# Feed-forward of an attention, mixture-of-experts and feed-forward kernel: VectorE and ScalarE take GpSimd's elementwise work, and the decoding is spread over more steps

## The chip, the cores and the metric

One core of a Trainium2 chip. The core has TensorE (matmuls), VectorE (DVE), ScalarE (ACT), GpSimd (POOL) and SyncE (SP, which only starts transfers here); each runs its own queue of instructions in order, and they wait for each other by semaphores. The metric is the device time of one execution in microseconds (us), as the median of the runs.

## The reference

Everything is float32. An attention (2 batches, 8 heads, 1152 keys, 576 pooled queries, width 64) gives 1152 tokens of 512. A routed layer sends each token to one of 8 experts. Its output goes through a feed-forward layer, the only stage that the change touches:

```python
def _moe2_ref(x, w_in, w_out):        # x 1152x512, w_in 512x2048, w_out 2048x512
    h = x @ w_in
    g = np.maximum(h, 0.0) + np.log1p(np.exp(-np.abs(h)))
    return (g @ w_out).astype(np.float32)
```

`w_in` and `w_out` reach the kernel as float64 words, which it decodes to float32 by integer operations.

## The kernel before

**Precision.** Each float32 operand is kept as two parts, `hi` (rounded for the matmul) and `lo` (the rest). `mm3` (L1450) makes one product with three matmuls: hi by hi, hi by lo, lo by hi. To split a weight tile of 128 x 1024, `split_unit` (L1363) lets ScalarE copy it to `hi` (L1370) and another engine subtract that from the tile to get `lo` (L1371); which engine, the caller says.

**Steps.** The feed-forward is a loop over 48 steps (L1831): two halves `hf` of the hidden width, three groups `g` of 384 tokens, eight columns `f` of 128 hidden units. In step n TensorE runs `h_unit` of step n (twelve matmuls of 384 columns into `fh`, three buffers) and `out_unit` of step n - 3 (nine matmuls of 512 columns into `fo`; LAG is 3). In steps 0 to 2 there is only `fh`. The softplus of a step needs, in the order of the queues:
- `softplus` (L1723): ScalarE `Abs` of `fh` into `ex` (L1726, one buffer), `Exp` (L1727), then u1 = 1 + ex on VectorE (L1729, `u` in the profile, one buffer);
- `g_split` (L1742) of the step before: ScalarE copies `ln` to `gH` (L1746), VectorE subtracts to get `gL` (L1747); TensorE's `out_unit` reads both;
- `softplus2` (L1732): ScalarE `Ln` of u1 (L1735), VectorE L1737 to L1739 (the error of u1, its subtraction, and the maximum with `fh`, which frees the buffer of `fh`).

After every eighth column `evac` copies `fo` to the five `part` tiles (first half) or adds it to them and scatters the rows to the output (second half, GpSimd, L700).

**Side work.** The rest is a list `side` of pairs of a due time (in steps) and a piece of work; after each step the loop issues all pieces that are due (L1843). So a piece's due time sets its place in every engine's queue:
- `split` of the last three early units (L1818), due at `WO_AT`, `lo` on GpSimd;
- 16 pieces of `w_in` and `w_out` of 128 x 512 words, at t = LATE0 + m x LATED: `late_load` at t - 3 (SyncE; it takes a buffer of a pool of eight, which words, `late` units and `part` tiles share), `late0` at t (ScalarE `Abs`, L1789, and a maximum on GpSimd, L1790), `late1` at t + 1 (three integer operations on VectorE, L1799 to L1801);
- `late_split` of the eight units so made (two pieces each), LATE2 steps after a unit's second piece, and for units 5 to 7 not before LATE3, LATE3 + 1.5, LATE3 + 3; `lo` on GpSimd;
- `place` (nine scatters of token places by GpSimd, due from step 18) and `tok_load` (step 27).

The earlier decoding of other weights, during the attention, has the same maximum on VectorE (L171).

Of the kernel before, what the change touches and what calls it, by code (L numbers as in the profile page):

```python
# [9 lines left out]
F32 = mybir.dt.float32  # L10
# [3 lines left out]
AF = mybir.ActivationFunctionType  # L14
# [7 lines left out]
def tile_attn_moe_ffn(  # L22
# [13 lines left out]
    nc = tc.nc  # L36
# [26 lines left out]
    NHIP = 4  # L63
    NHIP2 = 5
    LATE0 = 2.0
    LATED = 1.347
    LATE2 = 2.527
    LATE3 = 25.778
    LATES = 1.5
    WO_AT = (0.0, 1.0, 3.0)  # L70
    X0B = 3
# [126 lines left out]
    ff_units = []  # L198
# [4 lines left out]
    late_units = ff_units[N_EARLY:]  # L203
# [7 lines left out]
    right = {}  # L211
# [62 lines left out]
    lt = ap1.tile([P, NCH, H, E], F32, name="lt")  # L274
# [1088 lines left out]
    def split_unit(u, r, eng, pool=None, keep=None):  # L1363
        pool = pool or (hipA if u[0] in ("w2", "wo") or keep is not None else right["hip"])
        if keep is None or ("hi", keep) not in fixed:
            a = pool.tile([P, 1024], F32R, tag="hi", name="hi")
            b = pool.tile([P, 1024], F32R, tag="lo", name="lo")
        if keep is not None:
            a, b = fixed.setdefault(("hi", keep), (a, b) if ("hi", keep) not in fixed else None)
        nc.scalar.copy(a, r)  # L1370
        eng.tensor_tensor(b, r, a.bitcast(F32), op=ALU.subtract)  # L1371
        hi[u], lo[u] = a, b
# [333 lines left out]
    hip2 = ctx.enter_context(tc.tile_pool(name="hip2", bufs=NHIP2, reuse_waits="tile"))  # L1706
# [16 lines left out]
    def softplus(g, f):  # L1723
        t = fh.pop((g, f))
        ex = fp.tile([P, GT], F32, tag="ex", name="ex", bufs=1)
        nc.scalar.activation(ex, t, AF.Abs)  # L1726
        nc.scalar.activation(ex, ex, AF.Exp, scale=-1.0)  # L1727
        u1 = fp.tile([P, GT], F32, tag="u1", name="u1", bufs=1)
        nc.vector.tensor_scalar_add(u1, ex, 1.0)  # L1729
        sp[g, f] = t, ex, u1  # L1730

    def softplus2(g, f):  # L1732
# [17 lines left out]
    fo, part, lt = {}, {}, {}  # L1750
# [33 lines left out]
    def late0(m):  # L1784
        t = words[m]
        a = fp.tile([P, 512], I32, tag="dec_a", name="dec_a", bufs=2)
        w = t.rearrange("p (n w) -> p n w", w=2)
        dec[m] = a, w[:, :, 1], w[:, :, 0]
        nc.scalar.activation(a.bitcast(F32), w[:, :, 1].bitcast(F32), AF.Abs)  # L1789
        nc.gpsimd.tensor_scalar_max(a.bitcast(F32), a.bitcast(F32), 2.0 ** -15)  # L1790

    def late1(m):
        a, top, low = dec.pop(m)
# [8 lines left out]
                                       op1=ALU.bitwise_or)  # L1802

    def late_split(m):
        split_unit(late_units[m], lt.pop(m), nc.gpsimd, hip2 if m < NHIP2 else right["hip"])

    split(ff_units[4], nc.vector)
    seq = [(hf, g, hf * 8 + f) for hf in range(2) for g in range(NG) for f in range(8)]
# [5 lines left out]
    def fat(t, f, *a):  # L1814
        side.append((t, len(side), f, a))

    for m in range(5, N_EARLY):
        fat(WO_AT[m - 5], split, ff_units[m], nc.gpsimd)  # L1818
    for m in range(2 * len(late_units)):
        t = LATE0 + m * LATED  # L1820
        fat(max(t - 3, 0), late_load, m)
        fat(t, late0, m)
        fat(t + 1, late1, m)
    for m in range(len(late_units)):
        t = LATE0 + (2 * m + 1) * LATED + LATE2
        fat(t if m < NHIP2 else max(t, LATE3 + LATES * (m - NHIP2)), late_split, m)
    for c in range(NCH):
# [3 lines left out]
    for n in range(len(seq)):  # L1831
        h_unit(*seq[n][1:])
        if n >= LAG:
            out_unit(*seq[n - LAG], (2, 0, 1) if seq[n - LAG][2] % 8 == 7 else range(CPG))
        if n >= LAG:
            evac((2,), *seq[n - LAG])
        softplus(*seq[n][1:])
        if n:
            g_split(*seq[n - 1][1:])
        softplus2(*seq[n][1:])  # L1840
        if n >= LAG:
            evac((0, 1), *seq[n - LAG])
        while side and side[0][0] < n + 1:  # L1843
            _, _, f, a = side.pop(0)
            f(*a)
# [38 lines left out]
```

## Time and profile before

| | |
|---|---|
| median of 3 runs | 684.07 us (682.27 to 684.11) |
| profiled execution | 681.26 us |
| span of it, first to last instruction | 679.4 us |
| mean granted TensorE clock | 0.988 |
| busy in the span: PE, DVE, ACT, POOL | 627.0, 527.4, 383.8, 323.1 us |

PE is TensorE's matmuls, PEld its weight loads (one for each matmul, and they overlap). A group of instructions shows count, busy time and mean duration; "idle before, releaser" is the time that the engine stood before them and what ended it. `x <- y` means that x is computed from y.

### The profile page before, as it was taken

The page shows a single profiled execution, that of the slowest core. Times are in us where ns is not written, and L with a number is a line of the kernel's source. Part 1 is how long each engine was busy: PE and PEld are TensorE (multiplying, and loading weights), DVE is VectorE, ACT ScalarE, POOL GpSimd, SP SyncE. Part 2 cuts the span into 40 slices and gives each one's busy share as a digit, 9 for nine tenths or more (in the row PEclk, how much of TensorE's full clock was granted, in tenths as well). Part 3 has the DMA queues.
Part 4 walks back from the last instruction along what each step waited for, and adds up shares of the span by engine and source line. Part 5 has one row for each costly group of instructions (what it writes and reads, how often), then busy time and mean ns, then how long its engine had stood idle before and what let it go on. Part 6 is the DMA issues. An engine that isn't in the chain of part 4 may idle for free. (4 is left out here: it accounts for less than half of the span.)

```text
span 679.4 us, 11733 instructions
## 1 busy us (share of the span) xinstructions
PE 627.0 (92%) x3995; PEld 505.6 (74%) x3995; DVE 527.4 (78%) x1000; ACT 383.8 (56%) x865; POOL 323.1 (48%) x255
## 2 busy tenths in 40 slices
PE   6997999999998999988899999999989999999996
PEld 4664666666665766667888889998778778999995
DVE  6899878887988897788937544656999999877664
ACT  4656376667665676663535443555566655754441
POOL 3666676877676876458352100023544564402021
PEclk9999899999998999998999999999999999999999
DMA  5884557585846452049778979974212212001011
GB/s 156 200 211 125 181 143 238 168 245 163 234 116 184 117 150 78 20 152 308 229 262 293 368 256 319 324 257 157 66 59 64 92 34 29 2 1 46 1 47 46
DMA packets 65665, 104.34 MB, mean 154 GB/s; under 512 B 21720, under 2 KB 35928, under 8 KB 65600
## 3 DMA queue, kind: packets, MB, share of 16 engines
q1 hardware_dynamic: 63248, 96.72, 46.6%
q0 software_dynamic: 2352, 6.82, 2.8%
q8 instruction: 33, 0.54, 0.4%
q14 instruction: 32, 0.26, 0.1%
HBM read 75.26 MB, written 16.02 MB: 134 GB/s over the span
## 5 line engine op out<-in xcount | busy, mean ns | idle before, releaser
L513 POOL TENSOR_TENSOR acc<-acc,pt 128x512 f32<-128x512 f32 (+1 forms) x100 | 149.2, 1492 | 40.5 <-ACT pt L476 36.4
L476 ACT ACTIVATE pt<-st 128x256 f32<-128x256 f32 (+1 forms) x288 | 110.1, 412 | 60.4 <-PE st L474 50.7
L421 DVE TENSOR_REDUCE mxt<-mx 128x1 f32<-128x384 f32 (+1 forms) x213 | 107.2, 549 | 23.6 <-PE mx L420 22.2
L472 PE MATMUL st<-QA,KA 128*128 128x256 f32 (+1 forms) x288 | 93.1, 330 | 7.6 <-ACT pt L476 7.5
L474 PE MATMUL st<-QB,KB 128*128 128x256 f32 (+1 forms) x288 | 84.0, 297 | 1.2 <-ACT QB L452 0.9
L490 PE MATMUL pv<-pt,vn 128*64 128x256 f32 (+1 forms) x576 | 83.4, 424 | 1.3 <-ACT pt L476 1.3
L420 PE MATMUL mx<-KA,QA 128*128 128x384 f32 (+1 forms) x192 | 70.2, 385 | 8.2 <-DVE mxt L421 5.0
L472 PEld LDWEIGHTS st<-QA,KA 128*128 128x128 f32 x288 | 54.6, 190 | 20.2 <-ACT pt L476 17.5
L1451 PE MATMUL fh<-x2H,hi 128*128 128x384 f32 x192 | 66.3, 345 | 1.3 <-DVEq L1676 1.3
L1453 PE MATMUL fh<-x2H,lo 128*128 128x384 f32 x192 | 64.8, 337 | 0.0
L1452 PE MATMUL fh<-x2L,hi 128*128 128x384 f32 x192 | 64.7, 337 | 0.0
L1453 PE MATMUL fo<-hi,gL 128*128 128x512 f32 x144 | 57.2, 397 | 6.2 <-DVE gL L1747 6.2
L490 PEld LDWEIGHTS pv<-pt,vn 128*64 128x64 f32 x576 | 38.2, 140 | 29.8 <-issue 6.1
L1371 POOL TENSOR_TENSOR lo<-raw,hi 128x1024 fp32r<-128x1024 f32 x7 | 16.9, 2422 | 87.9 <-ACT hi L1370 87.9
L420 PEld LDWEIGHTS mx<-KA,QA 128*128 128x128 f32 (+1 forms) x192 | 35.4, 190 | 30.6 <-DVE mxt L421 13.7
L1452 PE MATMUL fo<-lo,gH 128*128 128x512 f32 x144 | 56.4, 392 | 0.0
L1451 PE MATMUL fo<-hi,gH 128*128 128x512 f32 x144 | 56.4, 392 | 0.0
L474 PEld LDWEIGHTS st<-QB,KB 128*128 128x128 f32 x288 | 54.7, 190 | 2.0 <-ACT QB L452 1.2
L1735 ACT ACTIVATE ln<-u 128x384 f32<-128x384 f32 x48 | 25.2, 525 | 44.1 <-DVE u L1729 43.8
L1371 DVE TENSOR_TENSOR lo<-raw,hi 128x1024 fp32r<-128x1024 f32 x37 | 44.2, 1221 | 7.6 <-ACT hi L1370 6.9
L1452 PE MATMUL y<-hL,hi 128*128 128x256 f32 x160 | 44.9, 280 | 2.4 <-DVE hL L1475 2.4
L1726 ACT ACTIVATE ex<-fh 128x384 f32<-128x384 f32 x48 | 23.5, 489 | 41.4 <-PE fh L1453 36.0
(332 smaller groups left out, 1572.2 us busy)
## 6 DMA issues: line engine op xcount, KB each, us to landing
raw<-in_moe_w_dram SPq DMA_DIRECT2D x72, 512.0 KB, 5.3
words<-in_moe_w_in_dram SPq DMA_DIRECT2D x16, 512.0 KB, 5.2
words<-in_moe_w_out_dram SPq DMA_DIRECT2D x16, 512.0 KB, 3.6
xs<-zt SPq DMA_DIRECT2D x13, 528.0 KB, 4.2
vn<-in_v_dram SPq DMA_DIRECT2D x8, 576.0 KB, 6.1
qn<-in_q_dram SPq DMA_DIRECT2D x16, 256.0 KB, 5.3
wf<-dec_o SPq DMA_DIRECT2D x16, 256.0 KB, 2.1
raw<-wf SPq DMA_DIRECT2D x8, 512.0 KB, 4.5
```

The source lines that it names most:

```text
L420: nc.tensor.matmul(m[0:n, 0:GT], QA[i][:, h, j * P:j * P + n], KA[i][:, h, x], start=True, stop=True)
L421: nc.vector.tensor_reduce(out=mxt[i][0:n, j, h, g:g + 1], in_=m[0:n, 0:GT], axis=AX.X, op=ALU.max)
L472: nc.tensor.matmul(st[:, 0:n], ka[:, h, c * P:(c + 1) * P], qa[:, h, q0:q1], start=True, stop=False)
L474: nc.tensor.matmul(st[:, 0:n], kb[:, h, c * P:(c + 1) * P], qb[:, h, q0:q1], start=False, stop=True)
L476: nc.scalar.activation(pt_t[s][:, h, 0:n], st[:, 0:n], AF.Exp)
L490: nc.tensor.matmul(o[h * 64:(h + 1) * 64, 0:n], vn[i][:, h, c - k, :], pt_t[s - k][:, h, 0:n], start=(c == k), stop=(c - k == NKC - 1))
L513: eng.tensor_tensor(a, a, pt_t[s][:, :, 0:n], op=ALU.add)
L1371: eng.tensor_tensor(b, r, a.bitcast(F32), op=ALU.subtract)
L1451: nc.tensor.matmul(o, a, b, start=first, stop=False)
L1452: nc.tensor.matmul(o, a, bl, start=False, stop=False)
L1453: nc.tensor.matmul(o, al, b, start=False, stop=last)
L1735: nc.scalar.activation(ln, u1, AF.Ln)
```

## The change

Four edits, all in the feed-forward stage. The `lo` subtraction of the three early units and of the eight late ones moves from GpSimd to VectorE, and so does the maximum of `late0`. The "plus one" of the softplus moves from VectorE to ScalarE. The decoding's pace LATED goes from 1.347 to 1.8 steps a piece, so that the last piece is due at step 29, not 22.2, and LATE3 goes from 25.778 to 24.2. The late units 5, 6 and 7 are then split at 24.3, 27.9 and 31.5 (before: 25.8, 27.3, 28.8).

```diff
-    LATED = 1.347
+    LATED = 1.8
-    LATE3 = 25.778
+    LATE3 = 24.2
...
-        nc.vector.tensor_scalar_add(u1, ex, 1.0)
+        nc.scalar.activation(u1, ex, AF.Copy, bias=1.0)
...
-        nc.gpsimd.tensor_scalar_max(a.bitcast(F32), a.bitcast(F32), 2.0 ** -15)
+        nc.vector.tensor_scalar_max(a.bitcast(F32), a.bitcast(F32), 2.0 ** -15)
...
-        split_unit(late_units[m], lt.pop(m), nc.gpsimd, hip2 if m < NHIP2 else right["hip"])
+        split_unit(late_units[m], lt.pop(m), nc.vector, hip2 if m < NHIP2 else right["hip"])
...
-        fat(WO_AT[m - 5], split, ff_units[m], nc.gpsimd)
+        fat(WO_AT[m - 5], split, ff_units[m], nc.vector)
```

## Rows read from the trace of the kernel before

**Rows 1.** Stretches of 20 steps each: length, then busy time by engine, clock, DMA.
```profile
480.05:574.48 94.43, 88.22 (x421) 74.06 (x420) 89.12 (x150) 53.92 (x103) 48.88 (x39) 1.00 0.23 62
578.64:662.68 84.04, 84.04 (x422) 76.12 (x420) 61.13 (x112) 44.09 (x89) 15.50 (x16) 1.00 0.06 20
```

**Rows 2.** Waits from 480.05 to 574.48: total us, times, longest us.
```profile
PEld fo L1453 <- DVE gL L1747: 9.4, 8, 1.8
PE fo L1453 <- DVE gL L1747: 6.2, 7, 1.3
PEld fh L1451 <- DVE ln L1739: 5.1, 13, 0.4
```

**Rows 3.** Groups of VectorE by line from 461.14 on.
```profile
L1738 DVE TENSOR_TENSOR ln<-ln,u 128x384 f32<-128x384 f32 x48 | 27.7, 576 | 1.7
L1739 DVE SCALAR_TENSOR_TENSOR ln<-fh,ln 128x384 f32<-128x384 f32 x48 | 26.8, 558 | 1.7
L1737 DVE SCALAR_TENSOR_TENSOR u<-u,ex 128x384 f32<-128x384 f32 x48 | 26.8, 557 | 3.8 <-ACT ln L1735 0.6
L1747 DVE TENSOR_TENSOR gL<-ln,gH 128x384 fp32r<-128x384 f32 x48 | 26.6, 554 | 2.8 <-ACT gH L1746 2.2
L1729 DVE TENSOR_SCALAR u<-ex 128x384 f32<-128x384 f32 x48 | 24.2, 504 | 20.4 <-ACT ex L1727 19.6
L1799 DVE TENSOR_SCALAR dec_a<-dec_a 128x512 int32<-128x512 int32 x16 | 17.6, 1097 | 0.0
L1800 DVE SCALAR_TENSOR_TENSOR dec_b<-words,dec_a 128x512 int32<-128x512 int32 x16 | 12.5, 783 | 0.5
L1801 DVE SCALAR_TENSOR_TENSOR late<-words,dec_b 128x512 int32<-128x512 int32 x16 | 11.1, 692 | 0.6
L1772 DVE COPY part<-fo 128x512 f32<-128x512 f32 x3 | 2.0, 681 | 0.0
```

**Rows 4.** Durations of two lines, least, median and most, in ns.
```profile
L1729 DVE TENSOR_SCALAR u<-ex x48: 350/360/1775, 464.6 to 666.1; 128x384 f32<-128x384 f32 x48
L171 DVE TENSOR_SCALAR dec_a<-dec_a x16: 408/934/1726, 33.7 to 275.8; 128x512 f32<-128x512 f32 x16
```

**Rows 5.** The order of time, GpSimd and VectorE: start us, duration us.
```profile
477.76 2.47 POOL L1371 TENSOR_TENSOR lo<-raw,hi 128x1024 fp32r<-128x1024 f32 x1 [1.19 <-ACT hi L1370]
...
478.48 2.04 DVE L1799 TENSOR_SCALAR dec_a<-dec_a 128x512 int32<-128x512 int32 x1
...
484.78 0.42 DVE L1799 TENSOR_SCALAR dec_a<-dec_a 128x512 int32<-128x512 int32 x1
```

**Rows 6.** Groups of VectorE and ScalarE from 461.14 on.
```profile
L1371 DVE TENSOR_TENSOR lo<-raw,hi 128x1024 fp32r<-128x1024 f32 x1 | 1.2, 1226 | 1.5 <-ACT hi L1370 1.5
...
L1727 ACT ACTIVATE ex<-ex 128x384 f32<-128x384 f32 x48 | 25.2, 525 | 1.6
L1746 ACT CAST gH<-ln 128x384 fp32r<-128x384 f32 x48 | 24.3, 506 | 4.2 <-DVE ln L1739 2.9
L1726 ACT ACTIVATE ex<-fh 128x384 f32<-128x384 f32 x48 | 23.5, 489 | 41.4 <-PE fh L1453 36.0 <-DVE u L1737 4.2
```

**Rows 7.** The order of time at the first step, TensorE and VectorE.
```profile
461.14 0.41 PE L1451 MATMUL fh<-x2H,hi 128*128 128x384 f32 x1 [1.26 <-DVEq L1676]
...
465.56 0.56 DVE L1737 SCALAR_TENSOR_TENSOR u<-u,ex 128x384 f32<-128x384 f32 x1 [0.59 <-ACT ln L1735]
```

**Rows 8.** The order of time in the tail, ScalarE, VectorE and TensorE.
```profile
666.47 0.53 ACT L1735 ACTIVATE ln<-u 128x384 f32<-128x384 f32 x1
...
669.42 0.56 DVE L1747 TENSOR_TENSOR gL<-ln,gH 128x384 fp32r<-128x384 f32 x1 [0.64 <-ACT gH L1746]
...
670.16 0.39 PE L1453 MATMUL fo<-hi,gL 128*128 128x512 f32 x1
```

**Rows 9.** DMA issues (KB each, median us to landing), and the only table load.
```profile
words<-in_moe_w_out_dram SPq DMA_DIRECT2D x8, 512.0 KB, 3.5
...
L89 ACT ACT_TABLE_LOAD  x1: 1283/1283/1283, 0.9 to 0.9; - x1
```

## The prediction

> **What bounds the kernel now.** I read the stretches first, then the waits, then the groups by line, then single instructions.
>
> The change touches only the feed-forward stage, 48 steps from 461.14 us on [rows 7]. One step of TensorE is twelve `fh` and nine `fo` matmuls, 21 weight loads. Both stretches of [rows 1] hold 420 weight loads, so both are 20 whole steps: 6 to 25 and 27 to 46, counted from 0. The first takes 94.43 us, the second 84.04 us, with the granted clock at 1.00, its upper level (2.4 GHz), in both. So 84.04 / 20 = 4.202 us is TensorE's own step, and steps 6 to 25 carry 94.43 - 84.04 = 10.39 us above it. That is all that this stage can give back: steps 0 to 5 (18.91 us) are three of `fh` alone and three of about 4.2, and steps 26 to 47 run at TensorE's pace already.
>
> What holds TensorE in steps 6 to 25? [Rows 2] name VectorE: `fo` waits for `gL` (9.4 us by the weight loads, 6.2 by the matmuls, overlapping), `fh` for `ln` (5.1 us). And VectorE is busy 89.12 of 94.43 us there, against 61.13 of 84.04 later [rows 1]. It is full, so the question is what it spends its time on.
>
> [Rows 3] show two groups whose mean is no property of the work. The softplus' "plus one" (L1729) has a mean of 504 ns, but 360 in the median and 1775 at most [rows 4]. The decoding's mask-and-shift (L1799) has a mean of 1097 ns. [Rows 5] show why: at 478.48 it starts while GpSimd's `lo` subtraction runs (477.76 to 480.23) and lasts 2.04 us, 0.29 beyond that one's end; at 484.78, with no subtraction running, it takes 0.42. So a one-input VectorE instruction that meets a GpSimd subtraction stands until it is over. The two-input ones hardly do: `gL` 554 and L1737 557 ns in the mean of 48 [rows 3].
>
> **The change, part by part.** VectorE first, in clean durations, in the 20 steps 6 to 25.
> - Softplus without the "plus one": 0.557 + 0.558 + 0.558 (L1738, clean value taken from its neighbours) + 0.554 = 2.227 a step [rows 3], 44.5 us.
> - Decoding, a piece every 1.8 steps, not 1.347: eleven pieces fall here, before all sixteen. L1799 0.42 [rows 5], L1800 0.69 (its mean of 0.783 holds stretched ones; I take that of L1801, which is of the same shape), L1801 0.692 [rows 3], and the maximum, now on VectorE. No row shows it in this stage; L171 is the same operation and shape, 0.408 at least, 0.934 in the median, 1.726 at most [rows 4], among GpSimd's attention work. I take 0.41, since GpSimd is left with scatters here and L1799 of this shape takes 0.42 beside light GpSimd work; 0.41 and 1.73 stay as ends. Piece 2.21, eleven 24.3 us.
> - Splits: VectorE's takes 1.226 [rows 6]. Six late ones here, 7.4 us. The three of `WO_AT` come in steps 0, 1 and 3.
> - Two copies of `part`, 0.681 each [rows 3]: 1.4 us.
>
> Sum 77.6 us, below TensorE's 84.04. VectorE stops being the bound, and the 10.39 us go.
>
> ScalarE takes the "plus one": 128x384 on it lasts 0.489 (`Abs`), 0.525 (`Exp`) or 0.506 (`gH`) [rows 6]; I take 0.51, ends 0.49 and 0.53. ScalarE was busy 53.92 us [rows 1]; 20 x 0.51 makes it at most 64.1 of 84.04, fewer with the pieces that move out. The Trainium skill, "ScalarE: Activation LUTs", What ACT_TABLE_LOAD costs, prices an activation with immediate bias at 186 ns + 0.833 per element, 506 ns here, and about 93 ns more where the bias is a pointer operand; by that the instruction would take 0.60, and the tail below would lose 0.09 us more; no row here has such a bias.
>
> *The new waits.* `u1` has one buffer, so ScalarE's write waits for L1738 of the step before, and behind it stand `gH` and `Ln`. But `Abs` of the same step already waits for L1737, and `Abs` and `Exp` (1.01 us) cover the 0.56 of L1738. VectorE in turn no longer waits for itself but for `Ln`: from one L1737 to the next goes 0.557 + 0.489 + 0.525 + 0.51 + 0.506 + 0.53 = 3.12 us, under 4.20.
>
> *The first steps* are where VectorE could still be late: three steps of `fh` alone pass at half length, and three splits fall there. Up to the end of `gL` of step 6 VectorE has 7 x 2.227 + 4 splits (4.9) + 3 maxima (1.2) + 3 x 1.81 = 27.1 us, from 465.6 [rows 7]: 492.7. I allow 1.2 more for its waits on ScalarE there (an estimate, about half of the 2.55 us of ScalarE's five instructions): 493.9. TensorE asks for it in step 9, since `fo` runs three steps behind: at 461.14 + 6.3 (the three short steps: 480.05 - 461.14 - 3 x 4.202) + 6 x 4.202 + 2.6 (twelve `fh` and two `fo`, an estimate: a little over half a step) = 495.2. It holds, with 1.3 us to spare; afterwards VectorE gains 0.3 us a step.
>
> *What moves.* Late loads and decoding go later. SP carries only these loads here, and they land in 3.5 us [rows 9], three steps (12.6 us) before `Abs` needs them. At step 26 the pool of eight is full (five `part`, two word tiles, one late unit), so the last load waits for the decoding of that step; it is needed in step 29, and it costs nothing. The last split, in step 31, ends 2.1 (`fh`) + 2.56 (ScalarE) + 1.67 (L1737 to L1739) + 1.23 = 7.6 us after that step's start, and is used in step 33, 2 x 4.2 + 2.1 = 10.5 us after it. GpSimd's nine placing scatters lose the maxima between them; their result is needed only from step 35.
>
> *The tail.* After the last `fh` nothing hides ScalarE: `Ln` [rows 8] comes 0.43 to 0.53 us later, since "plus one" ran on VectorE under `gH` and now stands in ScalarE's queue. `gL` ends 669.98 and its matmul starts at 670.16, so 0.18 is slack; I count +0.3 us.
>
> Sum: -10.4 + 0.3 = -10.1 us against the profiled execution's 681.26 (span 679.4): 671.2. The median of the runs shown is 684.07, 2.8 above it; the stage that changes is the same, so I forecast 684.07 - 10.1 = **674.0 us**.
>
> **Rivals.**
> - *VectorE stays the bound for a while.* For: only 1.3 us to spare at step 9. If the maximum costs L171's median of 0.934 [rows 4], eleven add 5.7 us: 83.3 of 84.04, so no catching up, and three early ones (1.6 us) overrun the 1.3. At its 1.73 eleven add 14.5: 92.1, and 2.3 us of the gain are left. Against: GpSimd has no tensor work left here. By the two prices 675 to 682, say 678.
> - *The change doesn't do what it says*, because it is not GpSimd that stretches VectorE. Then L1799 keeps its 1.097 and the maximum takes its 0.934: 77.6 + 7.4 + 5.7 = 90.7 for steps 6 to 25, and steps 26 to 31, which now decode too, only keep pace. Gain 94.43 - 90.7 - 0.3 = 3.4: 680.7. Against: [rows 5], where the long one ends with GpSimd's subtraction.
> - *Slower: ScalarE reloads its table at each "plus one".* One load took 1.283 us [rows 9]; away and back is 2.57 a step. ScalarE's step, 64.1 / 20 = 3.2, becomes 5.8 during the decoding and at least 5.1 after it: 32 x 5.8 + 16 x 5.1 = 267 us, where 209 pass now from 461.14 to the 670.16 of [rows 8]: 742. It decides from "plus one" above 1.5 us, where ScalarE's step passes 4.2. Against: the whole trace holds one table load [rows 9], among copies, `Abs`, `Exp` and `Ln`. The Trainium skill, "ScalarE: Activation LUTs", Table sets, says that cheap functions (copy, abs) are in every set; by that it does not happen, and the one load agrees.
>
> **Chances.** Forecast 0.83, with a range of its own of 671.2 to 677; VectorE early 0.08; not GpSimd 0.05; table loads 0.03; the rest, 0.01, lies anywhere. Within 0.3% (about what runs of this kernel can tell from no change, 2 us) only a part of the third case and of the rest falls: 0.03. Slower 0.04, faster 0.93. The range goes from 671.0, where every step is as short as step 26 (578.64 - 574.48 = 4.16 us between the stretches of [rows 1]), the tail loses nothing and a run falls somewhat below the median, to 679.0, through most of the first rival.
>
> **What would show it.** Right: steps 6 to 25 take 84 to 85 us; `fo` waits on `gL` for under 1 us there; L1799 has a mean near 0.42 and the maximum near 0.41; VectorE is about 92% busy in these steps; ScalarE's "plus one" lasts 0.49 to 0.53 (0.60 would be the pointer price); one table load. Wrong: a maximum or L1799 near 1 us without GpSimd (second rival); waits on `gL` between steps 6 and 12 (first rival); more table loads; or a word load that lands after `Abs` asks for it, which would show as ScalarE idle before L1789.

## The result, and the profile after

Right after the prediction the changed kernel took 674.35 us in the median of 4 runs (672.72 to 675.87), the kernel before beside it 684.09 (4 runs, 682.27 to 685.63): a ratio of 0.9858 (95% interval, as for all ratios here, 0.9830 to 0.9885). Twice more the same code ran beside the experiments: 681.88 us (11 runs, ratio 0.9952, 0.9929 to 0.9974) and 680.29 us (9 runs, 0.9929, 0.9898 to 0.9959). So the kernel is faster in all three, but by 9.7 us once and by 2.3 and 4.9 us later. Its 24 runs fall into two groups: 6 at 672.7 to 675.9, 18 at 678.7 to 683.4. The forecast of 674.0 lies in the smaller group; 17 of the 18 others lie above the range's 679.0. The reason, as far as one profile of the smaller group and two of the larger show it, is one thing that the prediction had dismissed, GpSimd's scatters; where they hurt differs from run to run.

The profiled execution of after took 675.87 us (span 674.1, mean granted clock 0.982), 5.39 below that of before. The feed-forward, from its first `fh` matmul to the start of its last `fo` matmul, went from 211.83 us (461.14 to 672.97) to 203.52 (463.87 to 667.39), 8.31 less; it began 2.73 us later, which is no delay: in the kernels below whose code is the same up to there and which show none it begins between 458.8 and 464.3.

Steps 6 to 25 of after, and the next 20 steps but one, in the columns of [rows 1]:

```profile
482.77:568.47 85.70, 83.42 (x422) 75.76 (x421) 76.14 (x140) 65.73 (x131) 1.06 (x1) 1.00 0.26 75
572.63:656.67 84.04, 84.04 (x422) 76.13 (x421) 55.04 (x100) 52.15 (x108) 6.96 (x12) 1.00 0.07 26
```

94.43 became 85.70, VectorE 89.12 became 76.14. The second stretch is as long as before, 84.04. The waits of the first stretch, to be held against [rows 2]:

```profile
POOL tok L981 <- DMA td<-tokid,pos: 17.3, 1, 17.3
ACT ex L1726 <- DVE u L1737: 12.8, 12, 2.0
DVE gL L1747 <- ACT gH L1746: 5.4, 7, 1.5
ACT dec_a L1789 <- DMA words<-in_moe_w_in_dram: 5.1, 1, 5.1
PEld fo L1451 <- ACT gH L1746: 2.6, 1, 2.6
...
PE fo L1451 <- ACT gH L1746: 2.3, 1, 2.3
```

The 9.4 us of `fo` on `gL` are gone. What is left of TensorE's waiting is one wait of 2.3 us on ScalarE's `gH`, and ScalarE had stood 5.1 us for a load of words. Least, median and most of the lines of [rows 4, 5], and of the new ones:

```profile
L1799 DVE TENSOR_SCALAR dec_a<-dec_a x16: 416/418/421, 481.5 to 591.7; 128x512 int32<-128x512 int32 x16
L1790 DVE TENSOR_SCALAR dec_a<-dec_a x16: 416/417/427, 476.7 to 588.1; 128x512 f32<-128x512 f32 x16
L1729 ACT ACTIVATE u<-ex x48: 522/525/532, 467.3 to 660.1; 128x384 f32<-128x384 f32 x48
```

None of these lines of VectorE is stretched any more. The one long step is step 6, 6.86 us. In the order of time, ScalarE and then TensorE:

```profile
484.72 0.66 ACT L1789 ACTIVATE dec_a<-words 128x512 f32<-128x512 f32 x1 [5.11 <-DMA words<-in_moe_w_in_dram]
...
486.77 0.49 ACT L1746 CAST gH<-ln 128x384 fp32r<-128x384 f32 x1
...
487.32 0.50 PE L1451 MATMUL fo<-hi,gH 128*128 128x512 f32 x1 [2.28 <-ACT gH L1746]
```

`Abs` of the words stands ahead of the softplus in ScalarE's queue, so `gH` came late. Why were the words late? GpSimd in order of time, the first and the last of its nine `td` scatters, and the DMA from 463.8 to 486:

```profile
457.21 1.09 POOL L700 DMA_INDIRECT td<-tokid,pos  x1 [1.86 <-DMA xs<-xn,slot]
...
468.12 0.97 POOL L700 DMA_INDIRECT td<-tokid,pos  x1 [0.80 <-DMA td<-tokid,pos]
```

```profile
DMA  0909000992967224138899961055694299995992
GB/s 1 30 0 15 15 0 15 52 30 7 30 15 22 7 7 22 15 89 295 355 429 392 207 22 37 22 44 74 96 74 74 103 118 118 104 103 59 96 81 22
...
words<-in_moe_w_in_dram SPq DMA_DIRECT2D x7, 512.0 KB, 19.6
```

In the kernel before, these scatters ran from 544.8 to 572.2, because GpSimd's subtractions and maxima stood in front of them. With these gone the queue was empty and they ran at 457, beside the first seven loads of words, which landed after 19.6 us in the median (4.6 in the same stretch of before). The DMA line is busy tenths in 40 slices: many slices are nine tenths busy at 15 to 118 GB/s, where others move 392 and 429.

The other group of runs has the delay elsewhere. The order of time around the stage's start in the third measurement of the same code (label e5_after), ScalarE, GpSimd's last scatter, TensorE (its last matmul ahead of the stage and the first in it), and then two stretches, the first 2.5 us of the stage and its steps 0 and 1:

```profile
458.21 0.37 ACT L1503 CAST x2H<-y 128x256 f32 x1 [1.37 <-PE y L1453]
466.85 0.37 ACT L1503 CAST x2H<-y 128x256 f32 x1 [8.27 <-remote]
...
465.76 0.96 POOL L700 DMA_INDIRECT td<-tokid,pos  x1 [0.21 <-issue]
...
460.54 0.28 PE L1453 MATMUL y<-hH,lo 128*128 128x256 f32 x1
468.10 0.66 PE L1451 MATMUL fh<-x2H,hi 128*128 128x384 f32 x1 [7.28 <-issue]
```

```profile
468.10:470.60 2.50, 2.50 (x8) 2.50 (x9) 1.22 (x1) 1.04 (x1) 0.00 (x0) 0.50 0.97 13
...
468.10:474.90 6.80, 6.80 (x25) 6.80 (x25) 1.62 (x2) 3.53 (x6) 0.00 (x0) 0.59 0.84 20
```

ScalarE's last copy ahead of the stage normally comes 2.42 us after the end of the one before it; here 8.27, so 5.85 us late. TensorE stood for 7.28 us and then ran at a granted clock of 0.50, the lower level (1.2 GHz), and 0.59 in the mean of steps 0 and 1, which took 6.80 us instead of 4.24 (e1_hold below). Its scatters ran from 455.42 to 466.72. Here the words still landed in time, and step 6 took 4.15 us. The trace of e0_after shows the same: 9.75 us instead of 2.42.

### The profile page after: what moved, and what is told of

Same layout as the page of the kernel before. It is cut to its first block, busy times and chain, and to the rows that moved or that the text cites. A ratio compares the mean times of both kernels' runs of the same rounds, so it can differ in the third digit from the quotient of the medians.

```text
span 674.1 us, 11763 instructions
## 1 busy us (share of the span) xinstructions
PE 624.1 (93%) x3995; PEld 509.8 (76%) x3995; DVE 507.6 (75%) x979; ACT 404.2 (60%) x913; POOL 267.8 (40%) x228
## 5 line engine op out<-in xcount | busy, mean ns | idle before, releaser
L421 DVE TENSOR_REDUCE mxt<-mx 128x1 f32<-128x384 f32 (+1 forms) x213 | 107.2, 548 | 21.7 <-PE mx L420 20.3
L490 PE MATMUL pv<-pt,vn 128*64 128x256 f32 (+1 forms) x576 | 82.0, 418 | 1.3 <-ACT pt L476 1.3
L700 POOL DMA_INDIRECT out_dram<-part,tok x9 | 9.3, 1037 | 172.1 <-DVE part L1777 171.5
L1371 DVE TENSOR_TENSOR lo<-raw,hi 128x1024 fp32r<-128x1024 f32 x40 | 47.9, 1222 | 7.8 <-ACT hi L1370 7.2
L1747 DVE TENSOR_TENSOR gL<-ln,gH 128x384 fp32r<-128x384 f32 x48 | 26.7, 556 | 35.9 <-ACT gH L1746 35.9
```

The lines of the kernel that those rows point to most:

```text
L421: nc.vector.tensor_reduce(out=mxt[i][0:n, j, h, g:g + 1], in_=m[0:n, 0:GT], axis=AX.X, op=ALU.max)
L490: nc.tensor.matmul(o[h * 64:(h + 1) * 64, 0:n], vn[i][:, h, c - k, :], pt_t[s - k][:, h, 0:n], start=(c == k), stop=(c - k == NKC - 1))
L1747: nc.vector.tensor_tensor(b, ln, a.bitcast(F32), op=ALU.subtract)
```

## The experiments

The kernels ran in three groups, each with the kernel before beside it (684.19, 684.21 and 685.2 us). "Stage" is the span from the first `fh` to the last `fo` matmul's start in the profile; the loss or gain is read there first, since the time ahead of the stage varies by some us.

**e0_after, e5_after: the changed kernel itself.**

> The changed kernel once more, beside the variants below. Both theories: ratio to before about 0.986; the feed-forward stage (first fh to last fo matmul) about 203.5 us, step 6 about 6.9 us long with ScalarE waiting some 5 us for a word load, the word loads of w_in landing some 20 us after issue.

681.88 us; stage 202.48. It missed: ScalarE stood for no load of words, but 7.3 us longer than normal ahead of the stage (9.75 less 2.42), as in the trace just shown.

> The changed kernel once more, unchanged, to see which of its two delays it has here. Theory A (the scatters freed early collide with loads wherever they are then): either ScalarE waits for words in step 6 (a stage of 203 to 204 us, 673 to 676 us) or the stage begins 8 to 10 us late at the branch ahead of it (679 to 683 us); in both the scatters lie at 454 to 470 us, and the kernel with GpSimd's maxima in the same call is faster by 3 to 11 us. Rival B (the difference between the two medians so far is the chip's, not the kernel's): the kernel before moves by the same amount, and the ratio is that of the kernel with GpSimd's maxima within 0.3%.

680.29 us; stage 203.19, started 5.85 us late. The kernel before moved by 1.0 us only, and the kernel with GpSimd's maxima beside it (e4 below) took 673.49, so the second median is no drift of the chip.

**e1_hold: the scatters held back.**

```diff
+    def hold():
+        nc.gpsimd.tensor_copy(dm, held_by[0][0:1, 0:1])   # reads one number of step 18's ln
+    fat(TD0, hold)
     for c in range(NCH):
         fat(TD0 + 0.6 * c, place, c)
```

> The changed kernel, with one small GpSimd copy of a value that VectorE makes in step 18 ahead of the nine placing scatters, so that they can't run before that step. Theory A (the scatters, no longer behind GpSimd's tensor work, run at the stage's start and delay the word loads beside them): the word loads land in 4 to 6 us, ScalarE no longer waits for them, step 6 takes 4.15 us, the stage is 2.4 us shorter than in the changed kernel (about 201.1 us), ratio to before about 0.982. Theory B (the first word loads are late for another reason, such as their place in SyncE's queue): step 6 stays near 6.9 us and the stage near 203.5.

672.93 us (6 runs, 668.64 to 675.49), ratio 0.9828 (0.9795 to 0.9862); stage 200.78. GpSimd stood 85 us at this copy:

```profile
537.12 0.18 POOL L1830 COPY dm<-ln 1x1 f32<-1x1 f32 x1 [85.09 <-DVE ln L1740]
537.47 1.10 POOL L700 DMA_INDIRECT td<-tokid,pos  x1 [0.18 <-issue]
```

No step is long, no load makes ScalarE wait, and neither delay occurs. One instruction that only orders GpSimd's queue is worth 9.0 us against e0_after in the same group. None of the 30 runs of the six kernels whose scatters come late (e1, e2, e3, e4, p6, p7) takes more than 677.33 us; 18 of the 24 of after take 678.7 or more. The early scatters are the cause of both delays.

**e2_max_gp: the maxima back on GpSimd**, which then hold the scatters as before.

```diff
-        nc.vector.tensor_scalar_max(a.bitcast(F32), a.bitcast(F32), 2.0 ** -15)
+        nc.gpsimd.tensor_scalar_max(a.bitcast(F32), a.bitcast(F32), 2.0 ** -15)
```

> The changed kernel with the maxima of the decoding back on GpSimd. They stand ahead of the scatters in GpSimd's queue again. Theory A: no wait for words, step 6 near 4.2 us, the stage near 201 to 202 us. Theory B: as the changed kernel, 203.5. On the stretching of VectorE: if only GpSimd's two-input subtraction holds one-input VectorE work, L1799 has a mean of 0.42 to 0.6 us here; if any GpSimd tensor work does, it is near 1 us and VectorE becomes late (fo waits for gL by several us).

671.79 us, ratio 0.9807 (0.9782 to 0.9831), the lowest median of all, though its interval overlaps e1's; stage 200.81, scatters from 532.85. So this part of the change gains nothing, and by freeing the scatters it costs what they cost. L1799 stays at 419 ns in the median (642 at most), but that tests little, for it meets only one maximum here. Other instructions of VectorE that begin while GpSimd's maximum of 1.6 us runs are held for a part of it:

```profile
474.74 1.49 POOL L1790 TENSOR_SCALAR dec_a<-dec_a 128x512 f32<-128x512 f32 x1 [20.24 <-DVE u L1737]
474.76 1.01 DVE L1738 TENSOR_TENSOR ln<-ln,u 128x384 f32<-128x384 f32 x1
```

L1738 takes 1.01 us, not 0.56, and ends before the maximum does. VectorE has room for this here: no step gets longer.

**e3_hold_tail, e4_max_gp_tail: the last step's plus-one on VectorE**, on top of e1 and of e2.

```diff
+        if (g, f) == seq[-1][1:]:
+            nc.vector.tensor_scalar_add(u1, ex, 1.0)
+        else:
             nc.scalar.activation(u1, ex, AF.Copy, bias=1.0)
```

> As the variant that holds the scatters, and the plus one of the very last step alone is on VectorE again. Both theories of the tail: if ScalarE's extra instruction ahead of the last Ln costs the 0.3 to 0.44 us between the last h_unit and the end, these come back: from the last step's first fh to the last fo matmul 10.3 us, not 10.7; otherwise no difference to the variant that only holds the scatters. Total about 0.3 us below that variant.

> The changed kernel with the maxima back on GpSimd and the plus-one of the last step alone on VectorE. Theory A (the scatters must stay late, and the tail loses 0.4 us to ScalarE's queue): scatters from about 533 us, no wait of ScalarE for words, steps 6 to 25 in 83.0 to 83.2 us, the stage 200.3 to 200.6 us, about 671.4 us, ratio 0.979 to 0.982. Rival B (the tail's 0.4 us is no part of the time, since the last evacuations wait for something else): the stage as with the maxima alone, 200.8 us.

673.31 us (ratio 0.9833, 0.9809 to 0.9858) and 673.49 us (0.9825, 0.9797 to 0.9852). The stage fell to 200.36 and 200.38, so the 0.42 us of the tail comes back in both profiles; in the time it cannot be seen.

**p1_u1_only, p2_pace_only, p3_split_only: one part of the change alone**, in the kernel before: the plus-one on ScalarE; the two pace constants; the splits on VectorE (the diff's lines of each, and no others).

> The kernel before, with only the plus one of the softplus moved to ScalarE. GpSimd keeps its subtractions, so L1799 still meets them. Theory A (what bounds the stage is VectorE's load per step, and GpSimd's subtraction is a part of that load through the one-input instruction that meets it): VectorE's step is 2.227 + (1.10 + 0.78 + 0.69) / 1.347 = 4.14 us, just under TensorE's 4.15, so most of the gain comes from this part alone: stage 202 to 205 us (before 211.8), L1799 with a mean of 1.0 to 1.3. Theory C (the parts add up, each by the VectorE time it takes away: 20 x 0.36 to 0.50 us here): stage 204 to 205 and the other parts add the rest. If the stage stays above 208, VectorE's load is not what the sum made it.

> The kernel before, with only the decoding's pace and LATE3 changed (1.8 steps a piece). Theory A: VectorE's step is 2.227 + 0.50 + (1.10 + 0.78 + 0.69) / 1.8 = 4.16 us, about TensorE's 4.15, so this part alone gives most of the gain too: stage 202 to 206 us. Theory C: less VectorE work in steps 6 to 25 but the same work in all, spread over more steps: 5 pieces x 2.6 us less there, stage about 204 if nothing comes back in steps 26 to 31, 208 or more if it does.

> The kernel before, with only the eleven subtractions moved from GpSimd to VectorE; the maxima stay on GpSimd, pace and plus one as before. Theory A: no one-input VectorE instruction near 2.0 us any more, L1799 with a mean of 0.42 to 0.6, the plus one never above 0.6; VectorE's step is 2.227 + 0.36 + 1.80 / 1.347 + 1.226 / 2.694 = 4.38 us, still over TensorE's 4.15, so about 20 x 0.23 = 4.6 us of the loss stay: stage 204 to 207. Theory D (the long one-input instructions come from something else than GpSimd's subtraction, such as the maxima or ScalarE): L1799 keeps a mean near 1 us and the stage gets longer, 212 to 216, since VectorE has 13.5 us more to do.

| | time, us | ratio (95%) | stage | L1799 mean, ns |
|---|---|---|---|---|
| before | 684.2 | 1 | 211.83 | 1097 |
| plus-one | 682.81 | 0.9994 (0.9966 to 1.0023) | 212.58 | 1109 |
| pace | 683.85 | 1.0000 (0.9964 to 1.0036) | 213.09 | 953 |
| splits | 680.57 | 0.9959 (0.9934 to 0.9983) | 208.21 | 559 |

Theory A's 202 to 205 for the plus-one was wrong by far: alone it is worth nothing. VectorE's groups of that kernel show a part of the reason, and a line of ScalarE the larger part:

```profile
L1738 DVE TENSOR_TENSOR ln<-ln,u 128x384 f32<-128x384 f32 x48 | 33.3, 693 | 1.7
...
L1799 DVE TENSOR_SCALAR dec_a<-dec_a 128x512 int32<-128x512 int32 x16 | 17.7, 1109 | 0.0
...
569.59 0.66 ACT L1789 ACTIVATE dec_a<-words 128x512 f32<-128x512 f32 x1 [4.90 <-DMA words<-in_moe_w_out_dram]
```

GpSimd's subtractions are still there and now also hold L1738, whose two inputs both lie in SBUF (`fh` and `fo` lie in PSUM, the memory of TensorE's results; the other tiles here lie in SBUF): 693 ns in the mean instead of 576, 2.73 us at most. That makes step 3 1.76 us longer than before. The larger loss is the scatters once more: the last load of words was issued at 556.7, among them (544.2 to 573.0), and ScalarE stood for it until 569.59, so that step 25 took 8.06 us, 3.90 too many. With the tail's 0.43 these outweigh the 5.4 us that the other steps of 6 to 25 gained. With the pace alone, steps 6 to 25 fell from 94.43 to 89.59 us, but steps 27 to 46 rose from 84.04 to 90.02, the "comes back" of theory C; 3.7 us of it lie in step 33 (7.91 us), for which GpSimd's last subtraction ended too late:

```profile
PEld fo L1452 <- POOL lo L1371: 2.3, 1, 2.3
PE fo L1452 <- POOL lo L1371: 2.0, 1, 2.0
```

Only the splits alone gained, 3.6 us of stage, less than the 4.8 to 7.8 expected (204 to 207). No subtraction of GpSimd is left in that kernel, and VectorE is still busy for 85.57 of the 90.96 us of steps 6 to 25, now with its own work and the maxima's holding (L1799 meets seven of them and takes 0.42 to 1.12 us there):

```profile
488.08:579.04 90.96, 87.38 (x422) 74.18 (x421) 85.57 (x153) 55.48 (x108) 33.55 (x32) 1.00 0.24 53
```

Three gains of -0.75, -1.26 and 3.62 us add up to 1.6; with the scatters held, all parts together give 11.05. So they do not add up. (The maxima alone were not run.)

**p6_hold_split_gp, p7_hold_no_u1: one part undone**, in e1_hold: the splits back on GpSimd; the plus-one back on VectorE.

> The changed kernel with the scatters held until step 18, and the splits' subtractions back on GpSimd. Theory A (a GpSimd subtraction holds the VectorE instruction that meets it for up to 2 us): VectorE sheds 6 x 1.23 = 7.4 us in steps 6 to 25 and gains about 6 x 1.6 = 9.6 us of holding, 78.3 of 83.0, so it keeps up on the average: the stage 201 to 204 us, with single steps of 4.5 to 6 us beside the subtractions. Rival B (the edits' gains add up): the splits' part alone gave 3.6 us, so the stage is 204.4 us or more.

> The changed kernel with the scatters held until step 18, and the plus-one back on VectorE. Theory A (VectorE's clean sum decides): it is busy 76.1 + 20 x 0.36 = 83.3 us in steps 6 to 25, as much as TensorE's 83.0, and starts behind: the stage 201.5 to 204.5 us, so the plus-one is worth 1 to 4 us once the rest is done. Rival B (the plus-one is worth nothing, as when it was moved alone): the stage 200.3 to 200.9 us, the tail's 0.4 us included.

673.40 us (4 runs, ratio 0.9848, 0.9806 to 0.9890; stage 202.79) and 674.14 us (4 runs, 0.9849, 0.9818 to 0.9879; stage 202.42). Both stages are as theory A said, 2.01 and 1.64 us above e1 (2.06 for the second without the tail, which it gets back). So once the rest is done, the splits and the plus-one are worth 2 us of stage each, in one profile of each; the ratios, against e1's 0.9828, cannot tell them from nothing. Steps 6 to 25 of both, p6 and then p7:

```profile
480.60:563.56 82.96, 82.96 (x422) 75.90 (x420) 76.87 (x130) 60.22 (x121) 23.40 (x24) 1.00 0.28 64
```

```profile
479.77:563.47 83.70, 83.69 (x422) 75.68 (x421) 79.17 (x155) 52.47 (x100) 11.86 (x19) 1.00 0.29 63
```

In both VectorE is under TensorE's 83 us (p7's 79.17 is not the 83.3 of its theory A), and the steps run at TensorE's pace but for single stalls: steps 3 and 33 of p6 (5.92, 4.49 us), steps 16 and 33 of p7 (4.60, 5.65). In p7 the largest is step 33, outside the stretch that the theory named: TensorE waits 1.17 us for the last split's `lo`. Step 3 of p6 is one subtraction and one two-input instruction of VectorE, in the order of time:

```profile
468.77 2.39 POOL L1371 TENSOR_TENSOR lo<-raw,hi 128x1024 fp32r<-128x1024 f32 x1 [0.85 <-ACT hi L1370]
...
468.84 2.73 DVE L1739 TENSOR_TENSOR ln<-ln,u 128x384 f32<-128x384 f32 x1
```

(L1739 here is L1738 of before.) It ends at 471.57, 0.41 after GpSimd's end, and lasts 2.17 longer than its 0.56.

**d1_dummy: GpSimd kept busy to no purpose.** In e1_hold, two subtractions whose result nobody reads, beside each late split.

```diff
         split_unit(late_units[m], lt.pop(m), nc.vector, ...)
+        for _ in range(2):
+            nc.gpsimd.tensor_tensor(idle, right["H"][:, 0, 0:960].bitcast(F32), hi[late_units[m]][:, 0:960].bitcast(F32), op=ALU.subtract)
```

> The variant of the changed kernel that holds the scatters, with two idle subtractions (128 x 960, about 2.3 us each) on GpSimd added at each of the eight late splits; nothing uses their result. Theory A: one-input VectorE instructions (L1790's and L1799's successors in this kernel) that meet one last up to 2 us or more, in at least four of the steps with a split; all others stay at 0.42, and the two-input instructions stay within 0.1 us of 0.56 and 0.69; the stage is 0 to 2 us longer than 200.8, since VectorE has some slack. Theory D: all one-input instructions stay at 0.42 to 0.43.

694.59 us, ratio 1.0159 (1.0112 to 1.0205); stage 222.46, 21.7 us above e1. The expectation of 0 to 2 us was wrong by an order. The split on VectorE, here and (second fence) in e1:

```profile
L1371 DVE TENSOR_TENSOR lo<-late,hi 128x1024 fp32r<-128x1024 f32 x8 | 23.3, 2912 | 0.0
```

```profile
L1371 DVE TENSOR_TENSOR lo<-late,hi 128x1024 fp32r<-128x1024 f32 x8 | 9.7, 1215 | 0.0
```

16 idle subtractions of 2.54 us stretch the eight splits from 1.22 to 2.91 us each, and the mask-and-shift (L1799, here L1802) to 0.81 in the mean; `fo` waits for `gL` again, 10.1 us in all. The expectation that two-input instructions stay as they are failed too: besides the splits, one `gL` took 2.58 us. It is the plainest proof that GpSimd's subtraction itself, without any data that someone needs, holds VectorE. That this alone was what the kernel before suffered from is not shown: p3 takes the subtractions away and keeps 7.4 of the 11.05 us, and p6 keeps them and is only 2.01 above e1. By these two, what filled VectorE was the sum of its own work and the holding.

## Why the prediction was right, and where it was wrong

*What bounds the kernel, and the size of the gain.* VectorE was the bound of steps 6 to 25, and it stopped being that: right. The size was off: TensorE's step is not 4.202 us. In e1 it takes 4.15 in steps 4 to 23, 4.16 to step 28, and later 4.22, but 4.16 in steps 35, 36, 43 and 44; the undisturbed steps of the other kernels do the same, except in d1 (4.19 early, 4.14 late). So [rows 1] gave the mean of later steps, and 20 earlier ones need 82.96 us, as e1 shows: 11.47 us could go, 1.08 more than the 10.39. The prediction had step 26 with its 4.16 and used it for the end of its range alone. Why some steps take 0.07 more was not tested.

*VectorE's sum.* 77.6 us forecast, 76.14 measured (75.71 in e1). L1799 0.42 and the maximum 0.41: 0.418 and 0.417. The first steps held: in steps 6 to 25 of e1, where nothing else delays them, TensorE never waits for VectorE. The rivals "VectorE stays the bound" and "not GpSimd" fall by this, the latter also by d1.

*"The two-input ones hardly do."* Wrong as a rule. L1738 with 2.73 us beside a subtraction of 2.39 (p6), and `lo` with 2.91 instead of 1.22 (d1), show that those with both inputs in SBUF are held as long. What misled the reading: in the kernel before none of these began inside a subtraction. The lines around the subtraction of [rows 5], in the order of time:

```profile
477.41 0.56 DVE L1738 TENSOR_TENSOR ln<-ln,u 128x384 f32<-128x384 f32 x1
477.76 2.47 POOL L1371 TENSOR_TENSOR lo<-raw,hi 128x1024 fp32r<-128x1024 f32 x1 [1.19 <-ACT hi L1370]
478.00 0.56 DVE L1739 SCALAR_TENSOR_TENSOR ln<-fh,ln 128x384 f32<-128x384 f32 x1
```

Beside all eleven subtractions of that trace L1738 had begun before, and kept its 0.56. L1739, one of whose inputs (`fh`) lies in PSUM, began inside all eleven and took 0.56 too, so for that kind the prediction was right. The Trainium skill, "SBUF — State Buffer", Who interferes with whom, says that a VectorE instruction with two SBUF inputs contends with a GpSimd instruction that reads SBUF, and that the order of issue decides who waits. The rows of p6 and d1, where the subtraction came first, and the L1738 shown here, which came first itself, agree; the prediction had read averages instead. It changed no term of the sum, since the subtractions left GpSimd, but it is a part of why the plus-one alone is worth nothing: the holding passes to the next in line that can be held.

*ScalarE's plus-one.* 0.51 forecast within 0.49 and 0.53; 0.526 measured, not the 0.60 of a pointer operand. One table load, so the slower rival falls.

*"What moves."* This is the step that failed. "GpSimd's nine placing scatters lose the maxima between them; their result is needed only from step 35" asked when the scatters are needed, not when they can start. Their due time, step 18, sets their place in GpSimd's queue and nothing else; with the work in front of them gone, they began 88 us earlier (457.21, not 544.8), into the loads of words. That the loads "land in 3.5 us" was the median of eight, seven of which were issued before the first scatter: 19.6 in the first trace, for the seven beside the scatters. The sign of it, ScalarE idle before L1789, was named, but priced at nothing.

*The tail.* +0.3 forecast, +0.43 measured, and 0.42 given back in e3.

*The sum of the first trace.* In steps 6 to 25, -10.39 forecast, -8.73 measured: 1.04 more from the shorter step (20 x 4.15 against 84.04) and 2.71 lost in step 6 (6.86 - 4.15). With the tail's +0.43 that is -8.30. Two errors of opposite sign left this only 1.8 us off the forecast -10.1, and the first four runs were all of the smaller group: that their median lies at 674.35 is luck. (It lies 9.7 us below that of before; where the 1.4 us beyond the stage's 8.3 lie is not shown.) In the larger group of runs the loss is 8 to 9 us: 5.85 or 7.3 of standing, and about 2.4 or 1.7 of slower first steps (the stages of e5 and e0 against e1's 200.78), which fits the 9.0 us between the medians of e0 and e1.

*Open.* What stood ahead of the stage. The profile calls what ScalarE waited for at L1503 remote, but the copy waits for one semaphore only, which TensorE's last `y` matmul raises. By the semaphore events of the traces it rises at 466.83 in e5 and 467.77 in e0, 6.0 and 7.6 us after the recorded end of that matmul (460.82 and 460.17); in after it rises 0.01 after it (462.60 after 462.59). So TensorE's signal was late, and not ScalarE; why is not shown. ScalarE goes on 0.1 and 1.7 us after GpSimd's last scatter instruction (466.85 after 466.72, 467.79 after 466.08), and with the scatters held it stands no longer than normal. A 16 KB transfer of an instruction queue took 3.78 and 3.11 us meanwhile, 1.25 in before, but 3.77 as well in the first trace of after, where ScalarE stood no longer than normal; so it does not settle it. Nor is it shown why one execution has the one delay and the next the other: the scatters start 3.16 and 3.25 us before the end of ScalarE's last copy but one where it stood, and 2.99 us before it where it did not, which hardly tells them apart.

## What to carry to other kernels

Taking work off an engine also takes away what held back the next work in its queue: ask when each later instruction of it can now start, and what it collides with, and hold it with a cheap dependence where early is worse. An instruction whose mean is stretched by another engine may be only the next in line: before you call other kinds free of it, look whether any of them ever began beside that engine's work (here L1739, with an input in PSUM, did and was free; L1738 never had, and was not). Take the stretched one away, and the holding can pass on, unless its cause goes. Read the floor of an engine from the very steps that are to speed up, and do not expect parts of a change to add up: the plus-one gained nothing alone, and undone at the end it costs some 2 us of stage.

## What the runs showed of the hardware that was not expected

- Nine scatters of 128 tokens' places, in packets of 4 and 32 bytes, stretched the landing of 512 KB loads from 4.6 to 19.6 us in the median; and in other executions TensorE's last signal ahead of the stage came 6.0 and 7.6 us late, until 0.1 and 1.7 us after GpSimd's last scatter instruction.
- GpSimd's subtraction of 2.4 us held a VectorE instruction of 0.56 us with both inputs in SBUF for 2.17 us (p6), but not L1739, which has one in PSUM (0.56 beside eleven subtractions in before); its maximum of 1.6 us, a one-input instruction, held L1738 for 0.45 us only (e2).
- After 7.28 us of standing, TensorE began the stage at a granted clock of 0.50, and its first two steps took 6.80 us instead of 4.24 (e5 against e1).
